# Batch operands of a seven-product layer: their order, their pairing, and one quarter summed in place

## The chip, the cores and the metric

The kernel runs on one core of a Trainium2 chip. Its metric is the device time of one execution in microseconds (us). The engines are named as in the profile: PE is TensorE (PEld its weight loads), DVE is VectorE, ACT is ScalarE, POOL is GpSimd, SP is SyncE, which issues most DMAs. Each engine works through its own list of instructions in order; they wait for each other by semaphores.

## The reference

Three layers follow each other. First an attention in two steps over 4 batches, 8 heads, 576 positions and 64 channels, then two feed-forward layers on 2304 tokens of 512 channels:

```python
p_packed = sm_attn(p, k, v)              # 32 packed queries per head
out = sm_attn(q, p_packed, p_packed)
x = out.transpose(0, 2, 1, 3).reshape(2304, 512)
h = x @ w_in                              # 512 x 2048
x = (np.maximum(h, 0) + np.log1p(np.exp(-np.abs(h)))) @ w_out
gate = 1 / (1 + np.exp(-(x @ w_gate)))    # 512 x 1536, "the second layer"
val = x @ w_val
return (gate * val) @ w_out2
```

All is float32. The kernel makes a float32 product out of three faster ones: every operand is split into a high part (a rounded copy) and a low part (the operand minus its high part), and high x high, high x low and low x high are summed.

## The kernel before, in words

**Stages.** Attention units and the first layer overlap from the start; the first layer ends at about 436 us of the profile, and the second layer fills the rest. Its input is `xa`, the first layer's sum, kept in SBUF transposed: per batch two halves of 288 positions (x1, x2), each with 512 channels.

**The second layer as seven products.** Gate and value are not computed as two products of 512 channels. Per batch the input is cut into four quarters of 256 channels x 288 positions, A11 and A12 (the two channel halves of x1), A21 and A22 (of x2), and the weights likewise; seven products of 256 channels are formed instead of eight (Winograd's variant of Strassen's method). On the input side it needs seven operands: A11, A12, A22, and the sums S1 = A21 + A22, S2 = S1 - A11, S3 = A11 - A21, S4 = A12 - S2. A21 itself is in no product. Each operand is 128 x 576 (two blocks of 128 channels by 288 positions).

**Making the operands.** `prep_A(b)` is a generator; each `yield` ends one step. A quarter is "split": ACT copies it to the high part (line 698), then DVE (for A22 POOL) subtracts to get the low part (line 99). A sum is one DVE instruction (line 705) into a tile `sum`, of which there is one buffer. Operands are allocated in pairs, one tile for both high parts and one for both low parts, the pairs being (A11, A12), (A22, S1), (S2, S3) and S4 alone. The tiles of batches 2 and 3 take the places of those of batches 0 and 1, and a tile is free only when both operands in it have had their last product.

**The loops.** `ps` is 0 for batches 0 and 1, then 1 for batches 2 and 3; inside, `f` runs over 12 slices of the hidden channels. `emit_gv` forms the seven products for each f in the order A11, S2, S3, S1, A12, A22, S4. Per operand and batch a product is 6 matmuls of 288 columns (lines 111 to 113), so one f is 84. The results gather in three PSUM banks (`ps_m`, pairs of banks); DVE adds them (lines 927 and 939) and each bank is free again only when DVE or ACT has read it. `emit_out2` is the last product: per pair of slices nine blocks of 6 matmuls of 512 columns (lines 974 to 976), each added into `xa` by DVE (line 982); two PSUM tiles serve these. After the last pair of each `ps` the sums go out by DMA (line 991).

**What sets the order.** Work that prepares later stages hangs in a queue `jobs`, and each call of `tick()` (after every product and block) takes one step from its front. `prep_B` makes the weight operands of the next f: DVE converts the raw weights in three steps each (lines 178, 183, 187), ACT and POOL split them. `prep_A(0)` and `prep_A(1)` enter the queue near the end of the first layer. The last f of ps 0 is run batch by batch: when batch 0's products are emitted, `prep_A(2)` goes to the front of the queue, and after batch 1's, `prep_A(3)` goes to the front, ahead of what is left of `prep_A(2)`. A scheduler then fixes every engine's list: it moves instructions forward past others where data and buffers allow. So `sum` of batch 2 already stands at 437 us, and the place of an instruction follows from both.

The stretch from about 616 to 655 us, in which ps 0 ends and the operands of batches 2 and 3 are made, is called the turn below.

Of the kernel before, what the change touches and what calls it, by code (L numbers as in the profile page):

```python
# [9 lines left out]
F32 = mybir.dt.float32  # L10
# [3 lines left out]
ALU = mybir.AluOpType  # L14
# [6 lines left out]
def attn_moe_moe_kernel(  # L21
# [21 lines left out]
    nc = tc.nc  # L43
# [5 lines left out]
    P = 128  # L49
# [241 lines left out]
    SPL = []  # L291
    SP0 = []
    ALO = ['A22']
    EV2 = EM2 = EM1 = [nc.vector, nc.vector]
    EGL = [nc.gpsimd, nc.vector]
    HIA = [5, 9]
# [382 lines left out]
    HB = B // 2  # L679
    Aop, Bop, scratch, gv = {}, {}, {}, {}  # L680

    def prep_A(b):
        pool = w2[0] if b % 2 == 0 else big
        n = 11 if pool is big else 7
        Aop[b] = {}
        for nms in (("A11", "A12"), ("A22", "S1"), ("S2", "S3"), ("S4",)):
            tiles = [
                pool.tile([P, 2, 2, HS], F32R, tag="big", bufs=n, name="aop")
                for _ in range(len(nms))
            ]  # L690
            for e, nm in enumerate(nms):
                Aop[b][nm] = [tiles[0][:, e], tiles[-1][:, 1 if len(nms) == 1 else e]]
        x11, x12 = x2(b, 0)[:, :2], x2(b, 0)[:, 2:]
        x21, x22 = x2(b, 1)[:, :2], x2(b, 1)[:, 2:]

        def split(nm, x):
            hi, lo = Aop[b][nm]
            nc.scalar.activation(hi, x, AF.Copy)
            split_lo(nc.gpsimd if nm in ALO else nc.vector, lo, x, hi)

        def sum_():
            return w2[0].tile([P, 2, HS], F32, tag="sum", name="sum")

        def tt(to, x, y, op):
            nc.vector.tensor_tensor(to, x, y, op=op)

        split("A11", x11)
        yield
        split("A12", x12)
        yield  # L710
        split("A22", x22)
        yield
        t = sum_()
        tt(t, x21, x22, ALU.add)
        yield
        split("S1", t)
        yield
        tt(t, t, x11, ALU.subtract)
        yield
        split("S2", t)  # L720
        yield
        tt(t, x12, t, ALU.subtract)
        yield
        split("S4", t)
        yield
        t = sum_()
        tt(t, x11, x21, ALU.subtract)
        yield
        split("S3", t)
        yield  # L730


# [99 lines left out]
    for i, (b, c) in enumerate(entries):  # L832
        if c == 0:
            while not att_done(2 * b + 1):
                att_tick()
            if b:
                for cc in range(2):
                    jobs.appendleft((f"wp{b}{1 - cc}", prep_wp_one(b, 1 - cc)))
        if (b, c) == (3, 0):
            jobs.append(("win2", prep_win(2)))  # L840
        if (b, c) == (3, 1):
            jobs.append(("wp02", prep_wp_two(0, 2)))
        if c >= 2 and b % 2 == 0:
            k = groups.index((b // 2, c))
            if k == 0:
                jobs.append(("wo2", prep_wo(2)))
            if k + 1 < len(groups):
                x, cc = groups[k + 1]
                jobs.append((f"wp{2 * x}{cc}", prep_wp_two(x, cc)))
            if k + 2 < len(groups) and weights and groups[k + 2][1] == weights[0]:  # L850
                cc = weights.popleft()
                jobs.extend(idle)
                idle.clear()
                jobs.append((f"win{cc}", prep_win(cc)))
                jobs.append((f"wo{cc}", prep_wo(cc)))
                idle.append((f"early{cc}", prep_early(early_in.get(cc, ()))))
            if (b, c) == BAT:
                jobs.extend(idle)
                idle.clear()
                jobs.append(("B00", prep_B(0, 0)))  # L860
        for x in range(2):
            if (b, c) == (x + 2, NCH1 - 2):
                jobs.append((f"A{x}", prep_A(x)))
        if (b, c) == CPC:
            cps[0] = CPS > 0
        if (b, c) == (1, 2):
            att.release()
            w2.append(tc.alloc_tile_pool(name="w2", bufs=1, side="right"))
        finish(f"wp{b}{c}" if c < 2 else f"wp{b - b % 2}{c}")
        for s in range(2):  # L870
            emit_h(b, c, s)
            pace = 0
            for bb in range(b + 1, B if c < 2 else 0):
                slots = 3 * (4 * bb - 2 * i - s) - MARGIN
                pace = max(pace, -(-att_left(2 * bb + 1) // max(1, slots)))
            ticks = [pace] * 3
            if len(pend) == DEPTH:
                emit_out1(*pend.popleft(), ticks)
            else:
                for m in range(KD):  # L880
                    between(m, ticks)
            pend.append((b, c, s))
# [119 lines left out]
    for i, (ps, f) in enumerate(steps):  # L1002
        finish(f"B{ps}{f}")
        if i + 1 < len(steps):
            n_ps, n_f = steps[i + 1]
            jobs.append((f"B{n_ps}{n_f}", prep_B(n_ps, n_f)))
        whole = list(range(HB))
        first_last = f in (SPL if ps else (SP0 + [NF - 1]))
        for n, group in enumerate([[p] for p in whole] if first_last else [whole]):
# [46 lines left out]
```

## Time and profile before

| what | value |
| --- | --- |
| median of three runs (lowest, highest) | 868.61 us (866.66, 870.32) |
| the profiled execution, its span | 866.77 us, 864.7 us |
| busy: PE, DVE, POOL, ACT | 839.6, 614.6, 473.2, 401.1 us |
| granted TensorE clock, mean | 1.000 of full speed |
| HBM read, written | 65.67 MB, 18.87 MB |

The span runs from the first to the last instruction; 2.07 us of the profiled time lie outside it. Busy times are of the engine's own instructions. A matmul's modelled duration is longer than the distance to the next one, since matmuls are pipelined: PE can count as busy while it loses time, and the loss is seen in the distances between starts. In the rows further down a line gives start, duration, engine, line of the kernel, operation, output tile <- input tiles, shapes and count.

### The profile page before, as it was taken

What the parts mean: (1) busy time and instruction counts of PE and PEld (TensorE: products, weight loads), DVE (VectorE), ACT (ScalarE), POOL (GpSimd) and SP (SyncE); (2) the same over time, 40 slices, a digit from 0 to 9 for tenths busy, and PEclk for the clock granted to TensorE, in tenths of its full rate; (3) what the DMA queues carried; (4) which work ended last, traced back from release to release, by engine and by line L of the source; (5) the groups of instructions that cost most, each with busy time, mean ns of one, the idle gap of its engine ahead of it and who ended that gap; (6) DMA issues with size and microseconds to landing.
All of it is one profiled execution on the core that took longest, in us unless ns stands there. A gap on an engine that the chain in (4) does not pass through costs nothing.

```text
span 864.7 us, 15615 instructions
## 1 busy us (share of the span) xinstructions
PE 839.6 (97%) x6100; PEld 789.6 (91%) x6100; DVE 614.6 (71%) x1047; ACT 401.1 (46%) x721; POOL 473.2 (55%) x455
## 2 busy tenths in 40 slices
PE   6899999999999999999999999999989999999997
PEld 5788999989999999999999999999869999999995
DVE  1875556757576767758898688897898756767665
ACT  4567565566666666677633422232342532322210
POOL 4454233346565545576479787796883634536400
PEclk9999999999999999999999999999999999999999
DMA  9983330113032402300057464554434212213004
GB/s 233 229 221 84 80 83 2 50 49 99 1 98 92 135 21 79 123 30 1 1 167 215 134 192 148 170 136 157 140 95 137 79 45 86 67 43 111 14 1 109
DMA packets 58009, 85.55 MB, mean 99 GB/s; under 512 B 6352, under 2 KB 39248, under 8 KB 57936
## 3 DMA queue, kind: packets, MB, share of 16 engines
q1 hardware_dynamic: 57648, 84.49, 34.5%
q8 instruction: 48, 0.79, 0.4%
q14 instruction: 25, 0.20, 0.1%
q10 hardware_dynamic: 288, 0.07, 0.0%
HBM read 65.67 MB, written 18.87 MB: 98 GB/s over the span
## 4 chain that ended last, share of the span: by engine, by line
PE 84%; DVE 7%; DMA 3%; ACT 2%; POOL 2%; issue 1%; SPq 0%; POOLq 0%; ACTq 0%; DVEq 0%
PE bank L113 9%; PE bank L111 9%; PE bank L112 9%; PE ps L650 7%; PE ps L651 7%; PE ps L653 7%; PE ps L976 5%; PE ps L975 5%; PE ps L974 5%; PE ps L113 4%; PE ps L111 4%; PE ps L112 4%; PE ps L587 2%; DVE aop L99 2%; PE ps L464 2%; PE ps L348 1%
## 5 line engine op out<-in xcount | busy, mean ns | idle before, releaser
L111 PE MATMUL bank<-aop,BH 128*128 128x288 f32 x672 | 198.7, 296 | 2.8 <-DVE work L927 1.1
L112 PE MATMUL bank<-aop,BH 128*128 128x288 f32 x672 | 197.9, 295 | 1.0 <-DVE aop L99 0.9
L113 PE MATMUL bank<-aop,BL 128*128 128x288 f32 x672 | 198.7, 296 | 0.1
L99 POOL TENSOR_TENSOR ghl<-g,ghl 128x576 fp32r<-128x576 f32 x64 | 93.7, 1464 | 131.5 <-ACT ghl L106 131.5
L658 DVE TENSOR_TENSOR xa<-xa,ps 128x288 f32<-128x288 f32 x224 | 98.1, 449 | 75.4 <-PE ps L653 75.3
L650 PE MATMUL ps<-ghl,woh 128*128 128x288 f32 x512 | 148.6, 305 | 1.6 <-DVE xa L658 1.5
L651 PE MATMUL ps<-ghl,wol 128*128 128x288 f32 x512 | 143.2, 295 | 0.0
L111 PEld LDWEIGHTS bank<-aop,BH 128*128 128x128 f32 x672 | 126.2, 188 | 8.0 <-issue 1.2
L112 PEld LDWEIGHTS bank<-aop,BH 128*128 128x128 f32 x672 | 126.4, 188 | 5.1 <-DVE aop L99 1.6
L113 PEld LDWEIGHTS bank<-aop,BL 128*128 128x128 f32 x672 | 126.5, 188 | 0.4 <-POOL BL L99 0.4
L99 POOL TENSOR_TENSOR BL<-cv,BH 128x512 fp32r<-128x512 f32 (+1 forms) x96 | 117.7, 1242 | 7.2 <-ACT BH L106 6.1
L653 PE MATMUL ps<-ghl,woh 128*128 128x288 f32 x512 | 109.1, 294 | 0.0
L650 PEld LDWEIGHTS ps<-ghl,woh 128*128 128x128 f32 x512 | 96.2, 188 | 4.1 <-DVE xa L658 1.3
L651 PEld LDWEIGHTS ps<-ghl,wol 128*128 128x128 f32 x512 | 96.3, 188 | 0.6
L927 DVE TENSOR_TENSOR work<-work,bank 128x576 f32<-128x576 f32 (+1 forms) x100 | 70.9, 724 | 28.6 <-PE bank L113 28.1
L974 PE MATMUL ps<-oh,gv 128*128 128x512 f32 x216 | 84.6, 392 | 1.3 <-DVE xa L982 0.8
L975 PE MATMUL ps<-ol,gv 128*128 128x512 f32 x216 | 84.8, 393 | 0.0
L976 PE MATMUL ps<-oh,gv 128*128 128x512 f32 x216 | 84.7, 393 | 0.0
L653 PEld LDWEIGHTS ps<-ghl,woh 128*128 128x128 f32 x512 | 82.2, 188 | 0.0
L982 DVE TENSOR_TENSOR xa<-xa,ps 128x512 f32<-128x512 f32 x90 | 61.5, 684 | 27.1 <-PE ps L976 26.6
L956 ACT ACTIVATE work<-bank 128x576 f32<-128x576 f32 (+1 forms) x25 | 15.8, 634 | 137.4 <-DVE bank L927 137.4
L113 PE MATMUL ps<-A2h,wpl 128*128 128x288 f32 x256 | 76.2, 297 | 2.4 <-POOL wpl L99 2.0
(123 smaller groups left out, 1743.6 us busy)
## 6 DMA issues: line engine op xcount, KB each, us to landing
cv<-B SPq DMA_DIRECT2D x52, 256.0 KB, 2.6
B<-cv SPq DMA_DIRECT2D x48, 256.0 KB, 3.8
raw_in<-in_moe_w_in_dram SPq DMA_DIRECT2D x16, 512.0 KB, 3.6
raw_out<-in_moe_w_out_dram SPq DMA_DIRECT2D x16, 512.0 KB, 3.6
raw_g<-in_moe_w_gate_dram SPq DMA_DIRECT2D x12, 512.0 KB, 4.2
raw_v<-in_moe_w_val_dram SPq DMA_DIRECT2D x12, 512.0 KB, 4.4
raw_o<-in_moe_w_out_dram SPq DMA_DIRECT2D x12, 512.0 KB, 4.1
xa<-in_q_dram SPq DMA_DIRECT2D x6, 576.0 KB, 6.5
```

The costliest lines, as they stand in the source:

```text
L99: eng.tensor_tensor(lo, x, hi.bitcast(F32), op=ALU.subtract)
L111: nc.tensor.matmul(ps, wh, xh, start=first, stop=False)
L112: nc.tensor.matmul(ps, wh, xl, start=False, stop=False)
L113: nc.tensor.matmul(ps, wl, xh, start=False, stop=last)
L650: nc.tensor.matmul(out_, wh[:, ms], gh[:, f], start=f == 0, stop=False)
L651: nc.tensor.matmul(out_, wl[:, ms], gh[:, f], start=False, stop=False)
L653: nc.tensor.matmul(out_, wo_hl[c, f][0][:, ms], gl[:, f], start=False, stop=f == 1)
L658: nc.vector.tensor_tensor(dst, dst, out_, op=ALU.add)
L927: nc.vector.tensor_tensor(to, x, y, op=ALU.add)
L974: nc.tensor.matmul(bank, gh[:, ts_], oh, start=f == 0, stop=False)
L975: nc.tensor.matmul(bank, gh[:, ts_], ol, start=False, stop=False)
L976: nc.tensor.matmul(bank, gl[:, ts_], oh, start=False, stop=f == 1)
```

## The change

Three things are altered in `prep_A`, and one is added.

- Before the splits a new generator `fold_A(b)` overwrites A21 in `xa` by two DVE instructions: A21 + A22, then minus A11. What stands there afterwards is S2.
- The operands are then made in the order A11, S2, S3, S1, A12, A22, S4, which is the order of the products. S2 is split from `xa` itself. The others come from it: S3 = A22 - S2, S1 = S2 + A11, S4 = A12 - S2, one DVE instruction each.
- The pairs are (A11, S2), (S3, S1), (A12, A22) and S4 alone.
- `fold_A(0)` and `fold_A(1)` enter the queue just ahead of `prep_A(0)` and `prep_A(1)`; `fold_A(2)` and `fold_A(3)` enter it at f = 3 and f = 5 of ps 0.

Per batch that is 2 folding sums and 3 sums where there were 4 sums; the splits are the same seven. The core of the diff:

```diff
+    FOLD = {3: 2, 5: 3}
+    def fold_A(b):
+        x11, x12, x21, x22 = quarters(b)
+        tt(x21, x21, x22, ALU.add)
+        yield
+        tt(x21, x21, x11, ALU.subtract)
+        yield
     def prep_A(b):
-        for nms in (("A11", "A12"), ("A22", "S1"), ("S2", "S3"), ("S4",)):
+        for nms in (("A11", "S2"), ("S3", "S1"), ("A12", "A22"), ("S4",)):
...
         split("A11", x11)
         yield
+        split("S2", s2)
+        yield
+        t = sum_(x22, s2, ALU.subtract)
+        yield
+        split("S3", t)
+        yield
+        t = sum_(s2, x11, ALU.add)
+        yield
+        split("S1", t)
+        yield
         split("A12", x12)
         yield
         split("A22", x22)
         yield
-        t = sum_()
-        tt(t, x21, x22, ALU.add)
-        yield
-        split("S1", t)
-        yield
-        tt(t, t, x11, ALU.subtract)
-        yield
-        split("S2", t)
-        yield
-        tt(t, x12, t, ALU.subtract)
+        t = sum_(x12, s2, ALU.subtract)
         yield
         split("S4", t)
-        yield
-        t = sum_()
-        tt(t, x11, x21, ALU.subtract)
-        yield
-        split("S3", t)
         yield
...
             if (b, c) == (x + 2, NCH1 - 2):
+                jobs.append((f"F{x}", fold_A(x)))
                 jobs.append((f"A{x}", prep_A(x)))
...
+        if ps == 0 and f in FOLD:
+            jobs.append((f"F{FOLD[f]}", fold_A(FOLD[f])))
```

In the lists that follow, a row is line, operation, output <- inputs and shape; line numbers of the changed kernel are higher by 1 to 13 (658 is 659, 705 is 688, 927 is 939, 939 is 951, 974 is 986, 982 is 994). First DVE's list at the end of the first layer, from the split of S4 of batch 1; `xa<-xa,ps` with a number adds one of the first layer's last blocks, `raw_g` is the first weight conversion of f = 1. Before:

```order
L99 TENSOR_TENSOR aop<-sum,aop 128x576
L658 TENSOR_TENSOR xa<-xa,ps_5441 128x288
L632 SCALAR_TENSOR_TENSOR g_5449<-ps_5405,t_5418 128x576
L705 TENSOR_TENSOR sum<-xa 128x576
L658 TENSOR_TENSOR xa<-xa,ps_5456 128x288
L658 TENSOR_TENSOR xa<-xa,ps_5466 128x288
L99 TENSOR_TENSOR aop<-sum,aop 128x576
L658 TENSOR_TENSOR xa<-xa,ps_5474 128x288
L658 TENSOR_TENSOR xa<-xa,ps_5482 128x288
L658 TENSOR_TENSOR xa<-xa,ps_5490 128x288
L658 TENSOR_TENSOR xa<-xa,ps_5498 128x288
L178 TENSOR_SCALAR ps_5556<-raw_g 128x512
```

And in the changed kernel, from the split of S1 of batch 1:

```order
L99 TENSOR_TENSOR aop<-sum,aop 128x576
L659 TENSOR_TENSOR xa<-xa,ps_5441 128x288
L633 SCALAR_TENSOR_TENSOR g_5449<-ps_5404,t_5417 128x576
L659 TENSOR_TENSOR xa<-xa,ps_5456 128x288
L659 TENSOR_TENSOR xa<-xa,ps_5466 128x288
L688 TENSOR_TENSOR sum<-xa 128x576
L99 TENSOR_TENSOR aop<-xa,aop 128x576
L659 TENSOR_TENSOR xa<-xa,ps_5476 128x288
L99 TENSOR_TENSOR aop<-sum,aop 128x576
L659 TENSOR_TENSOR xa<-xa,ps_5486 128x288
L659 TENSOR_TENSOR xa<-xa,ps_5494 128x288
L659 TENSOR_TENSOR xa<-xa,ps_5502 128x288
```

Behind the block 5441 the changed list has three sums or splits (S4's sum, A12, S4) where before has two (S3's sum, S3).

Next DVE's list inside the turn. `work` and `bank` are the sums of the products, `ps1` with a number is a block of the last product, `aop` an operand's tile. Before, the last rows up to the split of S3 of batch 2 (aop_7785), which is the last operand made; aop_7868 is S4 and aop_7867 S3 of batch 3:

```order
L705 TENSOR_TENSOR sum_7875<-xa_78,sum_7875 128x576
L927 TENSOR_TENSOR work_7931<-work_7908,bank_7932 128x576
L982 TENSOR_TENSOR xa_78<-xa_78,ps1_8096 128x512
L99 TENSOR_TENSOR aop_7868<-sum_7875,aop_7868 128x576
L982 TENSOR_TENSOR xa_78<-xa_78,ps1_8127 128x512
L705 TENSOR_TENSOR sum_7885<-xa_78 128x576
L982 TENSOR_TENSOR xa_78<-xa_78,ps1_8168 128x512
L99 TENSOR_TENSOR aop_7867<-sum_7885,aop_7866 128x576
L982 TENSOR_TENSOR xa_78<-xa_78,ps1_8194 128x512
L705 TENSOR_TENSOR sum_7892<-xa_78 128x576
L982 TENSOR_TENSOR xa_78<-xa_78,ps1_8220 128x512
L99 TENSOR_TENSOR aop_7785<-sum_7892,aop_7784 128x576
```

In the changed kernel, where aop_7874 holds S1, aop_7876 A12 and aop_7877 S4 of batch 3, and sum_7900 belongs to S4 of batch 2:

```order
L688 TENSOR_TENSOR sum_7886<-xa_78 128x576
L951 TENSOR_TENSOR work_7829<-work_7829,bank_7844 128x288
L939 TENSOR_TENSOR bank_7858<-work_7798,bank_7858 128x288
L99 TENSOR_TENSOR aop_7876<-xa_78,aop_7875 128x576
L951 TENSOR_TENSOR work_7842<-work_7842,bank_7858 128x288
L99 TENSOR_TENSOR aop_7874<-sum_7886,aop_7873 128x576
L688 TENSOR_TENSOR sum_7894<-xa_78 128x576
L939 TENSOR_TENSOR work_7939<-work_7916,bank_7940 128x576
L99 TENSOR_TENSOR aop_7877<-sum_7894,aop_7877 128x576
L939 TENSOR_TENSOR work_7958<-work_7939,bank_7959 128x576
L688 TENSOR_TENSOR sum_7900<-xa_78 128x576
L939 TENSOR_TENSOR work_7939<-work_7939,bank_7975 128x576
```

Before, five blocks of the last product (ps1) stand in these rows; now none does, and in their place stand the sums of the first products of ps 1: S2, S3 and S1 (bank_7940, bank_7959, bank_7975).

Last, PE's list at the turn. `bank<-aop` rows are the seven products, `ps1` rows the nine blocks of the last pair of ps 0. Before, behind the product S2 of batch 2 (aop_7784, aop_7785):

```order
L111 MATMUL bank_7932<-aop_7784,BH_7656 128x288
L112 MATMUL bank_7932<-aop_7785,BH_7656 128x288
L113 MATMUL bank_7932<-aop_7784,BL_7657 128x288
L976 MATMUL ps1_8012<-oh_7336,gv_7449 128x512
L974 MATMUL ps1_8012<-oh_7538,gv_7628 128x512
L975 MATMUL ps1_8012<-ol_7539,gv_7628 128x512
L976 MATMUL ps1_8012<-oh_7538,gv_7629 128x512
L974 MATMUL ps1_8040<-oh_7336,gv_7448 128x512
L975 MATMUL ps1_8040<-ol_7337,gv_7448 128x512
L976 MATMUL ps1_8040<-oh_7336,gv_7449 128x512
```

In the changed kernel, behind the product A22 of batch 3 (aop_7875, aop_7876):

```order
L111 MATMUL bank_8007<-aop_7875,BH_7664 128x288
L112 MATMUL bank_8007<-aop_7876,BH_7664 128x288
L113 MATMUL bank_8007<-aop_7875,BL_7665 128x288
L986 MATMUL ps1_8020<-oh_7546,gv_7636 128x512
L987 MATMUL ps1_8020<-ol_7547,gv_7636 128x512
L988 MATMUL ps1_8020<-oh_7546,gv_7637 128x512
L111 MATMUL bank_8035<-aop_7794,BH_7664 128x288
L112 MATMUL bank_8035<-aop_7794,BH_7664 128x288
L113 MATMUL bank_8035<-aop_7794,BL_7665 128x288
```

Before, 18 matmuls of ps 1 (A11 of both batches, S2 of batch 2) run, then all nine blocks with S2 of batch 3 between them, then S3 and the rest. In the changed list 72 matmuls of ps 1 (A11, S2, S3, S1, A12, A22, all for both batches) run with no block between them, then half a block, then S4; the other eight blocks stand behind that, spread over the products of f = 1. The 18 output DMAs of ps 0 follow their blocks: in SP's list they now stand among the loads of weights for f = 3 and f = 4 of ps 1, where before they stood in one piece ahead of these. DVE's two folding sums of batch 2 stand at the start of f = 0 of ps 0, those of batch 3 in f = 1 and f = 2, earlier than they enter the queue; the sum for S3 of batch 2 stands in f = 2, where before the sum for S1 of batch 2 stood at the start of f = 0.

## Rows read from the trace of the kernel before

**Rows 1.** The page's first part: busy time, share, instructions.
```profile
PE 839.6 (97%) x6100; PEld 789.6 (91%) x6100; DVE 614.6 (71%) x1047; ACT 401.1 (46%) x721; POOL 473.2 (55%) x455
```

**Rows 2.** PE's waits at the turn, 619 to 660 us: total, times, longest.
```profile
PE bank L111 <- DVE work L927: 1.1, 2, 0.8
PE bank L112 <- DVE aop L99: 0.9, 1, 0.9
PE ps L974 <- DVE xa L982: 0.8, 1, 0.8
PE bank L111 <- DVE work L939: 0.6, 1, 0.6
```

**Rows 3.** PE's waits at the first layer's end, 420 to 437 us.
```profile
PE ps L650 <- DVE xa L658: 1.5, 3, 0.6
PE bank L111 <- DVE xa L658: 0.7, 1, 0.7
```

**Rows 4.** PE's waits from 437 to 480 us.
```profile
PE bank L111 <- POOL ol L99: 0.5, 1, 0.5
```

**Rows 5.** PE matmuls with operand tiles by stretch: elapsed, busy (count), clock, DMA share, GB/s.
```profile
436.14:442.10 5.96, 5.96 (x46) 1.00 0.65 179
627.59:653.50 25.91, 10.32 (x66) 1.00 0.43 126
```

**Rows 6.** The same for matmuls of the last product, `gv`.
```profile
645.80:653.54 7.74, 7.73 (x34) 1.00 0.81 257
627.80:653.50 25.70, 13.00 (x54) 1.00 0.43 127
```

**Rows 7.** The same for the first layer's last blocks, `ghl`.
```profile
423.26:435.90 12.64, 10.46 (x72) 1.00 0.00 0
```

**Rows 8.** DVE groups by shape, 619 to 653.55 us: busy, mean ns, idle before.
```profile
L99 DVE TENSOR_TENSOR aop<-sum,aop 128x576 fp32r<-128x576 f32 x8 | 8.3, 1038 | 0.7 <-ACT aop L698 0.5
...
L99 DVE TENSOR_TENSOR aop<-xa,aop 128x576 fp32r<-128x576 f32 x4 | 5.7, 1434 | 0.1
L705 DVE TENSOR_TENSOR sum<-xa 128x576 f32<-128x576 f32 x3 | 3.3, 1110 | 0.0
...
L705 DVE TENSOR_TENSOR sum<-xa,sum 128x576 f32<-128x576 f32 x2 | 2.4, 1181 | 0.0
...
L705 DVE TENSOR_TENSOR sum<-sum,xa 128x576 f32<-128x576 f32 x2 | 1.5, 744 | 0.0
```

**Rows 9.** DVE's instructions in order of time, inside the turn.
```profile
616.82 0.45 DVE L927 TENSOR_TENSOR work<-work,bank 128x288 f32<-128x288 f32 x1 [0.20 <-PE bank L113]
...
636.86 0.44 DVE L939 TENSOR_TENSOR work<-work,bank 128x288 f32<-128x288 f32 x1
637.23 0.45 DVE L927 TENSOR_TENSOR bank<-work,bank 128x288 f32<-128x288 f32 x1
...
641.11 0.68 DVE L982 TENSOR_TENSOR xa<-xa,ps 128x512 f32<-128x512 f32 x1
641.71 0.74 DVE L705 TENSOR_TENSOR sum<-sum,xa 128x576 f32<-128x576 f32 x1
642.38 0.67 DVE L982 TENSOR_TENSOR xa<-xa,ps 128x512 f32<-128x512 f32 x1
643.20 1.78 DVE L99 TENSOR_TENSOR aop<-sum,aop 128x576 fp32r<-128x576 f32 x1 [0.15 <-ACT aop L698]
```

**Rows 10.** POOL's instruction that runs beside DVE's last one of rows 9.
```profile
643.09 1.28 POOL L99 TENSOR_TENSOR BL<-cv,BH 128x512 fp32r<-128x512 f32 x1
```

**Rows 11.** DVE groups at the first layer's end, 423.26 to 435.91 us.
```profile
L99 DVE TENSOR_TENSOR aop<-sum,aop 128x576 fp32r<-128x576 f32 x3 | 3.7, 1235 | 0.7 <-ACT aop L698 0.6
...
L183 DVE SCALAR_TENSOR_TENSOR ps<-raw_g,ps 128x512 int32<-128x512 int32 x1 | 0.7, 679 | 0.0
```

**Rows 12.** Busy by stretch: elapsed, then PE, PEld, DVE, ACT, POOL, clock, DMA share, GB/s.
```profile
436.00:460.00 24.00, 23.52 (x176) 23.31 (x177) 22.39 (x35) 8.77 (x13) 21.61 (x26) 1.00 0.69 200
460.00:600.00 140.00, 139.87 (x895) 130.51 (x895) 114.98 (x175) 40.67 (x66) 111.52 (x124) 1.00 0.56 164
```

More of the change, by code (lines that the diff above doesn't have):

```diff
@@ L680, in attn_moe_moe_kernel, with quarters, tt @@
     Aop, Bop, scratch, gv = {}, {}, {}, {}
+    def quarters(b):
+        x1, x2_ = x2(b, 0), x2(b, 1)
+        return x1[:, :2], x1[:, 2:], x2_[:, :2], x2_[:, 2:]
+    def tt(to, x, y, op):
+        nc.vector.tensor_tensor(to, x, y, op=op)
+    def fold_A(b):
[4 more added lines that the diff above has]
+        yield
     def prep_A(b):
@@ L692, in prep_A @@
                 Aop[b][nm] = [tiles[0][:, e], tiles[-1][:, 1 if len(nms) == 1 else e]]
-        x11, x12 = x2(b, 0)[:, :2], x2(b, 0)[:, 2:]
-        x21, x22 = x2(b, 1)[:, :2], x2(b, 1)[:, 2:]
+        x11, x12, s2, x22 = quarters(b)
         def split(nm, x):
@@ L699, in split, with sum_ @@
             split_lo(nc.gpsimd if nm in ALO else nc.vector, lo, x, hi)
[L701 to L705, printed above, removed]
+        def sum_(x, y, op):
+            t = w2[0].tile([P, 2, HS], F32, tag="sum", name="sum")
+            tt(t, x, y, op)
+            return t
         split("A11", x11)
+        yield
[8 more added lines that the diff above has]
+        split("S1", t)
         yield
```

## The prediction

> **What bounds the kernel now.** I read the page's first part, then PE's waits by stretch, then the distances between PE's starts, then DVE's groups where PE loses time. PE is busy 839.6 of 864.7 us and no other engine passes 71% [rows 1]: only time that PE loses can be won, and the change must win it where it acts. A matmul of 288 columns follows the one before in 5.96 / 45 = 0.1324 us (the 46th of that row was already running), one of 512 columns in 7.74 / 34 = 0.2276 [rows 5, 6]. With that I can say what a stretch needs. At the turn, from 627.59 to 653.55, PE runs 66 matmuls of seven products and 54 of the last product [rows 5, 6]: 66 x 0.1324 + 54 x 0.2276 = 21.0 us in 25.96, so 4.9 us are lost. The waits that the profile names there are all for DVE, 3.4 us together, and only one of 0.9 us is for an operand; the others are for banks and blocks that DVE has not yet read [rows 2]. At the first layer's end 72 matmuls need 9.5 us and take 12.65 until the first of the second layer starts [rows 7]: 3.1 lost, again to DVE [rows 3]. From 437 on one wait of 0.5 us is for POOL, at the first change of weights [rows 4]. So about 8.5 us lie where operands are made, and there DVE is the engine that is late.
>
> **The turn: what goes, what comes.** DVE makes 12 low parts (two more are POOL's) and 7 sums there now, in 21.2 us, the five groups summed [rows 8]. One of these by itself takes 0.74 and the next starts 0.67 later (641.71 to 642.38) [rows 9]. One that meets a POOL instruction takes far longer: the split of 643.20 ends at 644.98, 0.61 after POOL's instruction of 643.09 ended at 644.37 [rows 9, 10]. So DVE was held until POOL was through. Over the 19, the excess above 0.745 is 21.2 - 14.2 = 7.0 us, 0.37 each.
>
> The change leaves 17: both folding sums of batches 2 and 3 and the sum for S3 of batch 2 are made long before, and two of the old sums have gone. It also lets DVE begin earlier. A11 and S2 of batch 2 take the tiles of A11 and S2 of batch 0, and the product S2 has been read by 616.82 + 0.37 [rows 9], while the first split used to start behind two more products. Against that stands what PE's list now asks. Before, all nine blocks (12.3 us of PE) stood in front of the product S3 and covered the making of S1, S4 and S3. Now 72 matmuls of ps 1 and half a block run first. The blocks are not lost, but they come when the operands are no longer wanted.
>
> I work out when the last operand is ready. From 616.8 to the split of S4 of batch 2 DVE's list has 18 sums of half banks at 0.37 (636.86 to 637.23), 5 blocks at 0.60 (641.11 to 641.71), 4 sums of whole banks and 17 splits and sums at 0.67 each (a whole bank has an operand's 576 columns) [rows 9]: 6.7 + 3.0 + 2.7 + 11.4 = 23.8 us. I followed POOL's list beside it, holding each of the 17 until POOL's current instruction ends and POOL's until DVE's ends: 0.40 each, 6.8 us, and 0.6 of waits for ACT and PE. DVE is through at 616.8 + 31.2 = 648.0. PE wants that operand after batch 1's 42 matmuls, six of a block and 72 of ps 1: 627.59 + 5.6 + 1.4 + 9.5 = 644.1. The loss is 3.9 where it was 4.9: **-1.0 us**.
>
> The ends: if POOL never held DVE, it would be through at 641.2 and nothing would be lost, -4.9. If each of the 17 took the 1.434 us of the four slowest splits [rows 8], 0.69 above one alone, the excess is 11.7 and DVE is through at 652.9, a loss of 8.8, +3.9. I take the worked value, since it is nearest to the 0.37 of the 19 measured.
>
> A rule of the Trainium skill bears on this: SBUF — State Buffer, section "Who interferes with whom", says that a VectorE instruction with two SBUF inputs and a GpSimd instruction that reads SBUF exclude each other, whoever starts second waiting for the whole of the other. The trace agrees (644.37 and 644.98). It speaks against the change in one point: the folding sums have two SBUF inputs as well, so each can hold POOL or be held wherever it is put. Were it a plain slowdown, the mean of 0.37 would carry over, and DVE would be through at 616.8 + 23.8 + 6.3 + 0.6 = 647.5, the turn at -1.5 in place of -1.0.
>
> **The first layer's end.** For batches 0 and 1 the change adds one DVE instruction each (2 folds and 3 sums for 4 sums). Batch 0's falls where DVE has room. Of batch 1's work the folds and the first sum come early, but A12 and S4 are now split last: behind block 5441 stand three splits or sums where there were two, while one conversion step moves behind the last block. A split costs 1.235 there, one conversion step 0.68 [rows 11]: +0.6 for the last block. The third conversion step of the value weights, on which POOL's first run for f = 1 waits (the 0.5 of [rows 4]), has the full instruction more ahead of it, +1.2. PE can lose both only once: I take **+0.9**. The ends: the three splits in that stretch are partly held by POOL now, and if the new places avoid POOL, 3 x (1.235 - 0.745) = -1.5; if the three behind block 5441 are all held like the slowest kind [rows 8], 3 x 0.69 = +2.1.
>
> **Folds in f = 0 to 2.** Four folding sums and one sum in place of one sum: 4 x 0.67 = 2.7 us of DVE. From 460 to 600 DVE is busy 115 of 140 us and PE loses nothing to speak of, so two of them cost nothing; from 436 to 460 it is 22.4 of 24 [rows 12], so the two of batch 2 fit barely. I take **+0.2**, between 0 and 1.3 (two in full); if DVE's room were gone, each would delay a bank by 0.67.
>
> **Transfers.** Nothing is added. The 18 output DMAs of ps 0 now wait for blocks that run through f = 1 of ps 1, and the loads for f = 3 queue behind some of them. These weights are wanted only when f = 2 has run too, at least 84 x 0.1324 = 11 us after the last such block, and that cover hides them; without it, PE would wait for as much as a load is late.
>
> **Sum.** -1.0 + 0.9 + 0.2 = +0.1 on the profiled 866.77 us. Of this 864.7 is the span; the 2.07 outside stay. The median of the runs is 1.84 above the profiled one, so I forecast on its scale: 868.61 + 0.1 = **868.7 us**, and by the bounds of the likely terms (turn -2.5 to +1.5, the rest 0 to +2) 866.1 to 872.1.
>
> **The rivals.** *The turn is cured.* All of PE's waits at the turn are for DVE [rows 2]; with two sums fewer and an earlier start DVE might give its banks back in time. Then the 4.9 go, the first layer's end costs nothing, and +0.2 stays: 863.9 us. For it speaks that POOL has no more to do than before; against it that POOL must not hold DVE at all. *The cover is missed* (the other side). PE reaches S3 and S1 of batch 3 with no block to fill, and DVE is still held by POOL, every split 1.434: +3.9 + 0.9 + 0.2 = 873.6 us. It decides at the product S1 of batch 3: PE is there 627.59 + 5.6 + 0.7 + 42 x 0.1324 = 639.5 at the earliest, and each us that its split ends later is lost. For it speaks that four of 12 splits now take as long; against, that the others take 1.04. *The order is not what PE waits for.* Three of four waits are for banks, and a bank is freed by DVE's place in its list: the splits stand between the sums as before, and the loss stays 4.9, only elsewhere: 0 + 0.9 + 0.2 = 869.7 us.
>
> **How the numbers follow.** Forecast 0.52, order not the cause 0.20, turn cured 0.18, cover missed 0.10. What a measurement of this kernel can tell from no change is 0.5%, 4.3 us: faster is below 864.3, slower above 872.9. Only the cured turn reaches below, and with little to spare (0.14 of its 0.18); only the missed cover reaches above, with most of its share (0.08). That gives 0.14, 0.78 and 0.08. The range of eight in ten holds forecast and third rival, and reaches towards the cured turn: 864.0 to 872.2.
>
> **What would show it.** In the new trace PE should run the first six products of ps 1 in one piece from about 636, with waits for DVE of 3 to 5 us in all between 627 and 650, the last of them for the split of S4 or S1, and no block before 645. DVE's last split should end near 648, ahead of eight of the nine blocks instead of among them. At the first layer's end PE's first product should start up to 1 us later than 435.9. Wrong would be: no waits at the turn (cured), a single wait above 2 us before S3 or S1 (cover missed), a DVE idle at the turn, or a wait for weights in f = 2 to 4 of ps 1.

## The result, and the profile after

The changed kernel takes 873.35 us in the median of 6 runs (873.13 to 876.75), the kernel before 868.55 in the same comparison: a ratio of 1.0067, with a 95% interval of 1.0053 to 1.0080. It is slower, by 4.8 us, and lies above the range of 864.0 to 872.2. The profiled execution took 874.09 us, its span is 872.2.

The page's first part, the row that answers to [rows 1]:

```profile
PE 843.1 (97%) x6100; PEld 791.7 (91%) x6100; DVE 619.0 (71%) x1051; ACT 400.1 (46%) x721; POOL 476.1 (55%) x455
```

Totals do not show where the time went. I cut the second layer, and the last part of the first, at instructions that both kernels have: the sum `g` of the first layer that is the 20th from the last, ACT's copies of the bank of A11, and its sigmoids. The rows of these cuts, first before, then after (start, duration, engine, line; ACT's copy of an operand, line 698 before, is line 714 in the changed kernel):

```profile
328.43 0.75 DVE L632 SCALAR_TENSOR_TENSOR g<-ps,t 128x576 f32<-128x576 f32 x1
437.81 0.65 ACT L944 ACTIVATE work<-bank 128x576 f32<-128x576 f32 x1 [0.63 <-PE bank L113]
471.05 0.65 ACT L956 ACTIVATE work<-bank 128x576 f32<-128x576 f32 x1
600.15 0.65 ACT L944 ACTIVATE work<-bank 128x576 f32<-128x576 f32 x1 [1.90 <-PE bank L113]
840.18 0.65 ACT L956 ACTIVATE work<-bank 128x576 f32<-128x576 f32 x1 [10.62 <-DVE bank L927]
```

```profile
329.26 0.75 DVE L633 SCALAR_TENSOR_TENSOR g<-ps,t 128x576 f32<-128x576 f32 x1
444.61 0.65 ACT L956 ACTIVATE work<-bank 128x576 f32<-128x576 f32 x1 [8.79 <-PE bank L113]
481.10 0.65 ACT L968 ACTIVATE work<-bank 128x576 f32<-128x576 f32 x1 [1.23 <-DVE bank L939]
609.85 0.65 ACT L956 ACTIVATE work<-bank 128x576 f32<-128x576 f32 x1 [1.90 <-PE bank L113]
847.60 0.65 ACT L968 ACTIVATE work<-bank 128x576 f32<-128x576 f32 x1 [10.62 <-DVE bank L939]
```

These are the start of the first layer's end, the first product of the second layer (f = 0 of ps 0), the sigmoid of f = 2, the first product of f = 10, and the last sigmoid of ps 1. Before, the four stretches between them take 109.38, 33.24, 129.10 and 240.03 us; after, 115.35, 36.49, 128.75 and 237.75. So the first layer's end lost 5.97, f = 0 to 2 lost 3.25, f = 3 to 9 won 0.35, and the turn won 2.28. The sum is 6.6; 0.83 more lies ahead of the first cut. The medians differ by 4.8 and the two profiles by 7.3; run 12 below shows how far the part ahead of that cut varies by itself.

**The turn.** PE's waits from 619 to 670 us, the rows that answer to [rows 2]:

```profile
PE bank L111 <- ACT work L956: 0.6, 1, 0.6
PE ps L986 <- DVE xa L994: 0.5, 1, 0.5
PE bank L111 <- DVE work L939: 0.4, 1, 0.4
PE bank L112 <- DVE aop L99: 0.2, 1, 0.2
```

1.7 us where there were 3.4, and 0.2 of them for an operand; 0.6 is for ACT, the rest for DVE. I had forecast waits of 3 to 5 us. The turn does what the change says, and more of it than I forecast.

**The first layer's end.** PE's waits from 423 to 443 us, which answer to [rows 3], and the busy time of three stretches ahead of that, before and after (elapsed, then PE, PEld, DVE, ACT, POOL, granted clock):

```profile
PE ps L651 <- DVE xa L659: 1.7, 3, 0.8
PE ps L654 <- POOL ghl L99: 0.7, 1, 0.7
PE bank L111 <- DVE xa L659: 0.5, 1, 0.5
```

```profile
388.00:396.00 8.00, 8.00 (x57) 7.79 (x57) 7.25 (x10) 6.04 (x10) 5.23 (x3) 1.00 0.00 0
396.00:404.00 8.00, 8.00 (x63) 8.00 (x62) 7.54 (x13) 6.20 (x10) 4.67 (x4) 1.00 0.00 0
404.00:412.00 8.00, 8.00 (x63) 8.00 (x62) 5.01 (x11) 5.31 (x8) 4.29 (x4) 1.00 0.01 2
```

```profile
388.00:396.00 8.00, 8.00 (x59) 7.84 (x59) 7.50 (x12) 5.88 (x11) 2.73 (x2) 1.00 0.00 0
396.00:404.00 8.00, 6.51 (x48) 6.23 (x47) 7.97 (x11) 6.42 (x11) 6.25 (x6) 1.00 0.00 0
404.00:412.00 8.00, 6.88 (x51) 6.53 (x50) 7.15 (x10) 2.72 (x5) 4.16 (x3) 1.00 0.01 2
```

Before, DVE is busy 14.8 of the 16 us from 388 to 404 and rests after it, and PE runs through. After, DVE is full until 411 and PE lies idle 2.6 us. What DVE does there, and what POOL does beside it:

```profile
402.72 1.27 DVE L99 TENSOR_TENSOR aop<-sum,aop 128x576 fp32r<-128x576 f32 x1
403.92 3.74 DVE L688 TENSOR_TENSOR xa<-xa 128x576 f32<-128x576 f32 x2
...
407.95 0.75 DVE L688 TENSOR_TENSOR sum<-xa 128x576 f32<-128x576 f32 x1
...
409.35 0.74 DVE L633 SCALAR_TENSOR_TENSOR g<-ps,t 128x576 f32<-128x576 f32 x1
```

```profile
403.34 1.95 POOL L99 TENSOR_TENSOR ghl<-g,ghl 128x576 fp32r<-128x576 f32 x1
405.25 1.80 POOL L99 TENSOR_TENSOR wpl<-cv,wph 128x512 fp32r<-128x512 f32 x1
```

The two folding sums of batch 1 take 3.74 us, 1.87 each in the mean, where one alone takes 0.75. They end at 407.66, 0.61 after POOL's second instruction at 407.05: the same 0.61 as in the split of [rows 9, 10]. The sum `g` stands behind them in DVE's list; before, its counterpart came 5.78 us earlier (403.57), 4.95 when the 0.83 ahead of the first cut are taken off. ACT, POOL and PE wait for it in turn.

**The granted clock.** Five rows of the same view, 1 us each:

```profile
438.00:439.00 1.00, 0.16 (x3) 0.02 (x1) 1.00 (x3) 0.00 (x0) 0.00 (x0) 0.72 0.00 0
439.00:440.00 1.00, 1.00 (x4) 1.00 (x5) 1.00 (x3) 0.00 (x0) 0.00 (x0) 0.50 0.00 0
440.00:441.00 1.00, 1.00 (x6) 1.00 (x5) 0.19 (x2) 0.00 (x0) 0.00 (x0) 0.50 0.00 0
441.00:442.00 1.00, 1.00 (x6) 0.88 (x4) 0.88 (x2) 0.00 (x0) 0.00 (x0) 0.58 0.00 0
442.00:443.00 1.00, 0.45 (x3) 0.34 (x3) 0.84 (x2) 0.00 (x0) 0.00 (x0) 1.00 0.00 0
```

For the last blocks PE ran at 1.2 in place of 2.4 GHz. Its longest wait just before was 0.8 us (the waits above); of the 4 us from 435 to 439 it was busy for 2.0. The parts below full speed add up to 0.28 + 0.50 + 0.50 + 0.42 = 1.7 us. No stretch from 425 to 480 of the profile before has a clock below 1.00.

### The profile page after: what moved, and what is told of

It reads as the page before. It is cut to its first block, busy times and chain, and to the rows that moved or that the text cites. A ratio compares the mean times of both kernels' runs of the same rounds, so it can differ in the third digit from the quotient of the medians.

```text
span 872.2 us, 15622 instructions
## 1 busy us (share of the span) xinstructions
PE 843.1 (97%) x6100; PEld 791.7 (91%) x6100; DVE 619.0 (71%) x1051; ACT 400.1 (46%) x721; POOL 476.1 (55%) x455
```

## The experiments

For each run the table gives the median, the ratio to the kernel before, and how much longer than before the four stretches were (cut as above, from the run's own profile; the two clock columns give what the lower clock took in the first two stretches and in the last, summed as above, and are contained in the stretches).

| kernel | median us | ratio, 95% interval | first layer's end | f = 0 to 2 | f = 3 to 9 | turn to end | clock, first two | clock, turn |
| --- | --- | --- | --- | --- | --- | --- | --- | --- |
| changed | 873.35 | 1.0067 (1.0053 to 1.0080) | 5.97 | 3.25 | -0.35 | -2.28 | 1.70 | 0 |
| 1: 0, 1 old making, new pairs | 870.79 | 1.0022 (1.0013 to 1.0031) | 0.83 | 3.45 | -0.36 | -1.82 | 0 | 0 |
| 2: 2, 3 old making, new pairs | 877.00 | 1.0095 (1.0081 to 1.0110) | 5.69 | 1.31 | 0.34 | 1.90 | 1.71 | 1.71 |
| 3: old order in 0, 1 | 874.45 | 1.0078 (1.0056 to 1.0099) | 5.13 | 3.32 | -0.35 | -2.18 | 0 | 0 |
| 4: folds of 2, 3 late | 874.00 | 1.0058 (1.0041 to 1.0076) | 5.92 | 1.93 | 0.37 | -2.16 | 1.70 | 0 |
| 5: folds of 0, 1 on POOL | 878.41 | 1.0108 (1.0091 to 1.0126) | 9.20 | 3.02 | -0.29 | -2.15 | 1.70 | 0 |
| 6: folds of 1 later | 874.43 | 1.0068 (1.0055 to 1.0081) | 5.08 | 3.47 | -0.36 | -2.19 | 1.70 | 0 |
| 7: 0, 1 wholly old, folds late | 868.81 | 1.0001 (0.9991 to 1.0011) | 0.10 | 0.18 | 0.01 | 1.52 | 0 | 1.71 |
| 8: new pairs alone | 870.23 | 1.0026 (1.0014 to 1.0038) | 1.05 | -0.14 | 0.00 | 1.90 | 0 | 1.71 |
| 9: as 7, new pairs in 0 | 867.38 | 0.9987 (0.9968 to 1.0005) | 0.01 | 0.29 | 0.01 | -1.72 | 0 | 0 |
| 10: two-input dummies | 875.69 | 1.0080 (1.0053 to 1.0107) | 4.50 | 3.34 | 0.34 | -0.56 | 1.71 | 0 |
| 11: one-input dummies | 875.50 | 1.0076 (1.0046 to 1.0106) | 5.79 | 1.92 | 0.36 | -0.54 | 0 | 0 |
| 12: before once more | 871.10 (1 run) | | 0.02 | -0.06 | 0.00 | -0.03 | 0 | 0 |

Theory 1, from the two profiles: the first layer's end pays for the extra sums and the late splits of batches 0 and 1, f = 0 to 2 for the folds of batches 2 and 3, and the turn gains.

**Run 1, batches 0 and 1 made in the old way.**

```diff
-        split("A11", x11) ... split("S4", t)      # for batches 0 and 1
+        A11, A12, A22, t = A21 + A22: S1, t -= A11: S2, t = A12 - t: S4, t = A11 - A21: S3
-                jobs.append((f"F{x}", fold_A(x)))
```

> The order, sums and products of batches 2 and 3 as in the changed kernel, those of batches 0 and 1 as in the kernel before (four sums each, no folding beforehand, A12 and A22 split early); tiles paired as changed. Theory 1 (the loss is batches 0 and 1: about 5.8 us by the end of the first layer, 3.2 from the folding sums that stand in VectorE's list where it has no room, 2.6 from splits that are now last and meet GpSimd; the turn gains 2 to 3; the folds of batches 2 and 3 cost about 2 in the first f steps): 873.4 - 5.8 = 867.6 us, between 866.5 and 868.7; last block of the first layer within 1 us of 435.9. Rival (the first layer's difference in the one profile is run variation, the loss is in the second layer): 872 to 874, as the changed kernel.

The first layer's end fell from 5.97 to 0.83: the loss there belongs to batches 0 and 1, and is no variation from run to run. But the time is 870.8, not 867.6: f = 0 to 2 kept their whole loss although the layer ended in time, and I had put 2 on it.

**Run 2, batches 2 and 3 made in the old way, no folds for them.**

> Batches 0 and 1 as in the changed kernel, batches 2 and 3 with the order and sums of the kernel before and no folding beforehand for them (tiles paired as changed). Theory 1: the first layer's loss of 5.8 stays, the 2 us of the first f steps go, the turn loses 2 to 3 us more than the changed kernel: 873.4 - 2.0 + 2.5 = 873.9, between 872.8 and 875.2. Rival (the loss is in the second layer, through the folds of batches 2 and 3): 868 to 870.

Slower than the changed kernel, by more than expected. The first layer's loss stays. f = 0 to 2 lose 1.31 with no fold in them, so part of that loss comes from the late layer. And the turn is not as it was before but 1.9 worse, with the new pairs and the old order; I had overlooked that the pairs had stayed new. Of these 1.90 us 1.71 are lower clock, from 663 to 668 us: without it the turn would be 0.2 longer, near to what it was before.

**Run 3, the folds of batches 0 and 1, but their splits in the old order** (A11, A12, A22, S1, S2, S4, S3, the sums all from the folded A21).

> As the changed kernel, with the folding sums of batches 0 and 1 too, but these two batches' operands made in the old order (A11, A12, A22, S1, S2, S4, S3). It tells the extra and moved sums from the new order of the splits. Theory 1 (both count, 3.2 for the sums and 2.6 for the order): 873.4 - 2.6 = 870.8, between 869.8 and 871.8. Rival 'order alone': as with the old making throughout, 867.6. Rival 'sums alone': 873.4.

The rival "sums alone" (873.4) is the nearest: 5.13 against 5.97, the time the same as the changed kernel's within the intervals. The order of the splits is not the cause. The changed kernel's 5.97 holds 1.70 of lower clock and run 3's 5.13 none, so without it the new order is the shorter by 0.9.

**Run 4, the folds of batches 2 and 3 late.**

```diff
-    FOLD = {3: 2, 5: 3}
+    FOLD = {7: 2, 9: 3}            # and both instructions kept in program order
```

> As the changed kernel, with the folding sums of batches 2 and 3 pinned at f = 7 and f = 9 of ps 0, where PE loses nothing, in place of f = 0 to 2. Theory 1 (these folds cost about 2 us where they stand): 873.4 - 2.0 = 871.4, between 870.5 and 872.3, and no waits for DVE at 445 to 480 beyond 1.2 us. Rival (the loss of f = 0 to 2 comes from the first layer ending late and the converted weights with it, not from the folds): 873.4, no change.

f = 0 to 2 got 1.3 shorter, f = 3 to 9 got 0.7 longer (0.37 against -0.35), and the time did not change beyond its interval. PE's waits there were 0.9 for POOL's low part of the weights and 0.9 for DVE. With run 1, where the layer ended in time and the folds alone lost 3.45, and run 2, where there were no folds and 1.31 were lost: either cause is enough, and they don't add.

**Run 5, the folds of batches 0 and 1 made by POOL.**

```diff
-        tt(x21, x21, x22, ALU.add)
+        nc.gpsimd.tensor_tensor(x21, x21, x22, op=ALU.add)     # b < 2; the second likewise
```

> As the changed kernel, but the folding sums of batches 0 and 1 are made by GpSimd in place of VectorE (those of batches 2 and 3 stay). Theory 1 (the folding sums cost what they add to VectorE's time from 388 to 410, where it has no room: two-input work of 16.7 us there against 12.3 before, and 4.3 us of the 5.1 lost by the fourth g from the end): the first product of the second layer starts at most 2.5 us later than before, against 6.0; 873.4 - 4 = 869.4 us, between 868.4 and 871. Rival (GpSimd's own work, gh and the weights' low parts, is what the folds hold up, and it would now be later still): 873 or more.

Theory 1 missed. The rival's number came in (873 or more) and its mechanism did not: PE's only wait for POOL there is 0.7 us. The two POOL sums of batch 1 took 1.42 and 1.40 us, as those of batch 0 did, and yet the first layer lost 9.2, of them 1.70 by the clock. DVE's waits from 386 to 456 us of this run:

```profile
DVE sum L688 <- POOL xa L696: 9.5, 2, 5.1
DVE xa L659 <- PE ps L654: 7.8, 8, 1.9
```

DVE itself stood for 9.5 us at two sums that need the folded A21, with the blocks and the next `g` queued behind them. A fold that is late on another engine costs more here than a fold on DVE.

**Run 6, the same instructions, the folds of batch 1 some 20 places later in DVE's list.**

> As the changed kernel, with the same instructions, but the two folding sums of batch 1 pinned some 20 places later in VectorE's list, behind the g that they stood in front of, where VectorE has room (4.4 of 8 us busy at 412 to 420 in the changed kernel). Theory 1 (place, not number): the 3.3 us that are lost between the g at 401 and the one at 409 go, some come back at the last blocks, since all of batch 1's operands are made later: 873.4 - 2.5 = 870.9, between 870 and 872. Rival (the number of instructions decides, wherever they stand): 873.4.

At the `g` before which they had stood the loss was indeed gone (0.5 us there, against 4.95), but at the layer's end it had come back: 5.08. Of these 1.70 are again lower clock, now at 432 to 436. Without the lower clock it is 3.4 against 4.3, and the time is the changed kernel's, as the rival said. The run does not show that no place is free: DVE is busy only 9.2 of the 16 us from 404 to 420, but the folds ran at 419.80 and 421.18, at the head of eight us in which it is busy throughout. A place between 409 and 419 was not tried.

**Run 7, batches 0 and 1 as before in every point, folds of 2 and 3 late.**

> Batches 0 and 1 as in the kernel before in every point (order, sums, tiles paired); batches 2 and 3 as changed, with their folding sums pinned at f = 7 and 9. Theory 1: the first layer's end costs nothing (within 0.3 us of before), f = 0 to 2 at most 1, the pinned folds 0.4, the turn gains 1.5 to 2.3: 868.6 - 1 = 867.6, between 866.5 and 868.6, faster than both kernels. Rival (the turn's gain hangs on the tile pairs of batches 0 and 1: with the old ones the first tiles of batch 2 come free only after the product A12): 869 to 870.

The rival was right that the turn's gain hangs on the pairs; 868.81 lies between the two ranges, 0.2 from either. The losses of the first three stretches are gone, the pinned folds cost nothing (0.18 and 0.01), but the turn lost 1.52 in place of gaining. There PE waited for operands (1.3 for ACT's high part, 0.9 for DVE's low part): with A11 and A12 of batch 0 in one pair, batch 2's first tiles come free only after the product A12. Behind these waits the clock fell (1 us each, the granted clock is third from the end):

```profile
651.00:652.00 1.00, 0.60 (x3) 0.55 (x3) 1.00 (x3) 0.42 (x1) 0.00 (x0) 0.74 0.00 0
652.00:653.00 1.00, 1.00 (x6) 1.00 (x5) 0.66 (x1) 0.24 (x1) 0.00 (x0) 0.50 0.13 39
653.00:654.00 1.00, 1.00 (x6) 1.00 (x5) 0.00 (x0) 0.39 (x1) 0.00 (x0) 0.50 0.76 223
654.00:655.00 1.00, 1.00 (x4) 0.88 (x4) 0.51 (x1) 0.75 (x2) 0.62 (x1) 0.55 0.00 0
```

That is 0.26 + 0.50 + 0.50 + 0.45 = 1.71 us: without it the turn would be 0.2 shorter than before, hardly a gain and no loss. Five of the twelve runs have a mean granted clock of 1.000, and their median is 867.96 us, where that of the nine such runs of the kernel before in the same comparison is 867.53.

**Run 8, the pairing alone.**

```diff
-        for nms in (("A11", "A12"), ("A22", "S1"), ("S2", "S3"), ("S4",)):
+        for nms in (("A11", "S2"), ("S3", "S1"), ("A12", "A22"), ("S4",)):
```

> The kernel before with nothing but the new pairing of operands in tiles (A11 with S2, S3 with S1, A12 with A22), for all batches; order and sums as before, no folding beforehand. It tells what the pairing alone does. With the old making of batches 0 and 1 and the new pairs the first layer ended 0.8 us later; with the old order in batches 2 and 3 and the new pairs the turn lost 1.9 us more than before: 868.6 + 0.8 + 1.9 = 871.3, between 870.3 and 872.3. Rival (pairing has no cost of its own, those two came from the folding sums): 868.6.

The two stretches came as expected, 1.05 and 1.90, but the second for another reason: 1.71 of the 1.90 are lower clock, from 657 to 661 us. The time is just below the range. f = 0 to 2 lost nothing (-0.14), so the pairs do not cost there. In DVE's list the pairing moves one split of batch 1, A12, six places down: its tiles are now the fifth and sixth of the batch and no longer the first two.

**Run 9, put together from these.**

```diff
+        old = (("A11", "A12"), ("A22", "S1"), ("S2", "S3"), ("S4",))
+        for nms in (old if b == 1 else new):      # making of 0 and 1 as before, folds late
```

> Batches 0 and 1 made as in the kernel before (order, sums, no folding); batch 0's tiles paired as changed, batch 1's as before; batches 2 and 3 as changed, their folding sums pinned at f = 7 and 9. Theory 2 (after seven runs: the first layer's end pays for VectorE's added time and for batch 1's new pairs, f = 0 to 2 for the folds that stand there, and the turn's gain needs the tiles of A11 and S2 of batch 0 in one pair): first product of the second layer within 0.3 us of before, f = 0 to 2 within 0.3, the turn -2.3: 868.5 - 2.0 = 866.5, between 865.6 and 867.4. Rival (the turn's gain hangs on the pairs of batch 1 too): 868.5 to 870.

As expected in the first three stretches, 0.01, 0.29 and 0.01; the turn won 1.72 where 2.3 were expected. 867.38 against 868.10 in the same comparison, clearly below the changed kernel; below the kernel before by median, with an interval (0.9968 to 1.0005) that still holds no change.

**Runs 10 and 11, superfluous work where the folds are queued.**

```diff
+        tt(x21, x21, x21, ALU.max)                                   # run 10: twice for batches 0 and 1
+        nc.vector.tensor_scalar(x21, x21, 1.0, None, op0=ALU.mult)   # run 11: in its place
```

> The kernel before with two superfluous VectorE instructions each for batches 0 and 1, where the changed kernel queues its folding sums: in-place maxima of A21 with itself (two inputs from SBUF, 576 columns), which change no value. Theory 2 (VectorE has no room at the first layer's end, and each added instruction costs its time there with what GpSimd holds it): 4 x 1.25 (27.4 us over 22 instructions of this kind in the changed kernel) = 5.0 us by the first product of the second layer, 868.5 + 5.0 = 873.5, between 872 and 874.5. Rival (the changed kernel loses by where it puts the making of operands, not by added time): 868.5 to 869.5.

> As the run with the superfluous maxima, but in-place multiplications of A21 by one: one input from SBUF in place of two, the same 576 columns, two each for batches 0 and 1. Theory 2 with the hold: a one-input instruction is not held by GpSimd, so each costs 0.75 us at most and the four 3.0 or less: 871.5 or less, at least 1.5 below the run with two inputs. Rival (the hold does not matter, only the count): the same time as with two inputs.

Run 10: 4.50 at the first layer's end where 5.0 were expected (0.42 of them lower clock); what the time has beyond the range is f = 0 to 2 (3.34, of which 1.3 is the part of the lower clock that falls after 443.8), which I had left out. Run 11 did not come out lower, and my premise was wrong. One of its instructions alone takes 0.45 us, but two of the four took over three times that. DVE's rows, then POOL's:

```profile
391.14 0.45 DVE L695 TENSOR_SCALAR xa<-xa 128x576 f32<-128x576 f32 x1
...
405.31 1.55 DVE L693 TENSOR_SCALAR xa<-xa 128x576 f32<-128x576 f32 x1
406.90 1.58 DVE L695 TENSOR_SCALAR xa<-xa 128x576 f32<-128x576 f32 x1
```

```profile
404.75 1.80 POOL L99 TENSOR_TENSOR wpl<-cv,wph 128x512 fp32r<-128x512 f32 x1
406.51 1.65 POOL L99 TENSOR_TENSOR ghl<-g,ghl 128x576 fp32r<-128x576 f32 x1
```

They end 0.31 and 0.32 after POOL's ends (406.55 and 408.16): held like the others. The Trainium skill says so in SBUF — State Buffer, section "Who interferes with whom": a scalar operation with one input can run in a mode that takes the port shared with GpSimd, and is then shut out as well. The trace agrees, 0.45 against 1.55. So these two runs show that added DVE instructions are enough for the loss (no operand was moved or changed), but do not tell the hold from the count.

**Run 12, the kernel before once more.**

> The kernel before once more, for a second profile: which stretches vary from one execution to another by themselves. By each theory the distances from the sums g at the first layer's end to the end of the program are the same within 0.3 us, and what differs lies before them: 867 to 870.

All four stretches are the same within 0.06 us, yet the run is 871.1, above the range. All of its difference lies ahead of the first cut, 4.40 us, of which 1.71 are lower clock (182 to 187 us). So the stretches can be compared between single profiles, with the lower clock taken out where it falls into one; the totals of single profiles can't.

## Why the prediction was wrong

**The first layer's end was the step that failed: +0.9 forecast, bounds -1.5 to +2.1, 5.97 measured.** I wrote that batch 0's extra instruction "falls where DVE has room" and that batch 1's folds "come early". They did come early, and batch 0's landed at 388, batch 1's at 404, within and right behind a stretch in which DVE had no room: busy 14.8 of 16 us. I had opened only the stretch from 420 on [rows 3, 7, 11], in which the old kernel visibly waits, and had taken the stretch before it for free because PE lost nothing there. With DVE almost full, PE did not wait before, and did with the next instructions. The parts, by the runs and if they add up: the new pairs of batch 1 1.05 (run 8, and 0.01 where batch 1 kept the old ones, run 9); the folds about 4.1 (5.13 - 1.05, run 3; the dummies of run 10, with the old pairs, also cost 4.1 without their 0.42 of lower clock); the lower clock 1.70, for which my sum had no term; the new order about -0.9 (what is left). The price of an instruction was wrong too: I took 0.75 to 1.24. From 380 to the end of the layer the sums and splits take, in groups, before and after:

```profile
L99 DVE TENSOR_TENSOR aop<-sum,aop 128x576 fp32r<-128x576 f32 x8 | 8.2, 1024 | 3.0 <-ACT aop L698 2.9
L705 DVE TENSOR_TENSOR sum<-xa 128x576 f32<-128x576 f32 x5 | 4.7, 949 | 0.1
L99 DVE TENSOR_TENSOR aop<-xa,aop 128x576 fp32r<-128x576 f32 x4 | 4.5, 1144 | 1.4 <-ACT aop L698 1.4
L705 DVE TENSOR_TENSOR sum<-sum,xa 128x576 f32<-128x576 f32 x2 | 3.4, 1682 | 0.0
L705 DVE TENSOR_TENSOR sum<-xa,sum 128x576 f32<-128x576 f32 x2 | 2.4, 1180 | 0.0
```

```profile
L99 DVE TENSOR_TENSOR aop<-xa,aop 128x576 fp32r<-128x576 f32 x6 | 8.9, 1500 | 0.6 <-ACT aop L714 0.6
L688 DVE TENSOR_TENSOR xa<-xa 128x576 f32<-128x576 f32 x5 | 7.1, 1415 | 0.1
L99 DVE TENSOR_TENSOR aop<-sum,aop 128x576 fp32r<-128x576 f32 x6 | 6.6, 1108 | 0.8 <-ACT aop L714 0.6
L688 DVE TENSOR_TENSOR sum<-xa 128x576 f32<-128x576 f32 x6 | 5.4, 898 | 0.1
```

21 instructions and 23.2 us before, 23 and 28.0 after (one in each list is of batch 2). Two instructions more are 4.8 us more: 1.5 by their own length, 3.3 because the group was held longer (1.22 us in the mean against 1.10). It did not meet POOL more often: 12 end 0.60 to 0.62 us after an instruction of POOL in either profile, but they exceed 0.745 by 0.91 in the mean, where before it was 0.63.

**f = 0 to 2: +0.2 forecast, bounds 0 to 1.3, 3.25 measured.** I priced the folds as DVE time against DVE's idle time. What they hit is a chain that I had not followed: a raw weight is loaded again only when conversion steps on DVE are through, and SP issues the load behind stores of converted weights that wait for POOL. Up to f = 2 nothing but the folds and the pairs differ in run 1, and the pairs alone cost nothing there (run 8). In run 1 the conversion of a raw value weight starts 27.13 us after the stretch's first copy (438.83), before 25.08 after it (437.81), and the whole of DVE's list stands at its load, 2.08 us in place of 0.58. The issue on SP (before, it took 1.41 us by itself) and DVE's wait, before and run 1:

```profile
457.65 1.41 SPq L155 DMA_DIRECT2D raw_v<-in_moe_w_val_dram  x1
...
462.89 0.70 DVE L178 TENSOR_SCALAR ps<-raw_v 128x512 int32<-128x512 int32 x1 [0.58 <-DMA raw_v<-in_moe_w_val_dram]
```

```profile
461.38 0.39 SPq L155 DMA_DIRECT2D raw_v<-in_moe_w_val_dram  x1
...
465.96 0.69 DVE L178 TENSOR_SCALAR ps<-raw_v 128x512 int32<-128x512 int32 x1 [2.08 <-DMA raw_v<-in_moe_w_val_dram]
```

A late first layer goes with the same wait: runs 2, 4, 11 and 10, which have no fold there, lost 1.31, 1.93, 1.92 and (without the lower clock) 2.0 us, and DVE stood 1.7 to 2.7 us at this load in them, against 0.6 to 1.2 before and in runs 7, 8, 9 and 12. Why it is 1.3 in one and 2.0 in another, and why both causes together give no more than one, I did not settle.

**The turn: -1.0 forecast, bounds -4.9 to +3.9, -2.28 measured.** The direction and the steps held. PE runs the six products in one piece, no block comes among them, and DVE's last split starts at 655.07, which is 645.4 on the scale of before (minus the 9.70 by which f = 10 began later): it ends at 646.1, and I had 648.0. DVE was held less than the 0.40 per instruction that I took, 0.29 over the 17. The two parts of the change are worth nothing alone: the pairs with the old order lose 1.9 (runs 2 and 8), the order with the old pairs of batches 0 and 1 loses 1.5 (run 7), all three by 1.71 of lower clock, so that 0.2 more, 0.2 more and 0.2 less is left; both together win 1.7 to 2.3. (Runs 10 and 11 won 0.5 with nothing changed there: differences of that size are not resolved.)

**Transfers: 0 forecast.** Nothing at the turn waits for one, as the waits above show, and from 670 us to the end PE waits once, 0.4 us for ACT, as before. From 480 on the changed kernel shows no loss; f = 3 to 9 are 0.35 shorter, which the sum did not have.

**The rivals.** "The cover is missed" gave 873.6 us, next to the measured 873.35, and is wrong all the same: it asked for waits above 2 us before S3 or S1, and the longest at the turn is 0.6. A number alone does not bear out a mechanism. "The order is not what PE waits for" falls with the turn's gain; only two of the four kinds of wait in [rows 2] were for banks, and not three. None of the rivals put the loss where it was: two carried the same +0.9 and +0.2, and the cured turn put the first layer's end at nothing.

**What stays open.** The stretches of the one profile add up to 6.6 us, the medians to 4.8. The kernel before has 4.40 us of play ahead of the first cut by itself, and its profile lay 1.8 below its median. The lower clock does not fall in every run of the changed kernel, and is not needed for the loss: one of the six has a mean granted clock of 1.000, and it took 873.13 us. How often it falls the runs do not tell. Whether a later place of batch 1's folds would have been free was not tried. Whether run 9 beats the kernel before by the 0.1% of its median was not resolved.

## What to carry to other kernels

An engine that is as full in a stretch as DVE was here (14.8 of 16 us) has no room for more work, even where the engine behind it still shows no wait: read the busy share of every stretch into which a change moves work, not only of those that already wait. Price an added VectorE instruction by what such instructions take in that stretch, with what GpSimd holds them, and ask which load is issued only when the work behind it is done. An order of work and the sharing of its buffers are one change: neither half of this one gained at the turn, only both together did. And look at the granted clock of a stretch before giving its time to a cause: one drop was most of what each half seemed to lose.

## What the runs showed of the hardware

The VectorE sums and splits that took over 0.85 us from 380 us to the end of the first layer, 24 in the two profiles together, all ended 0.60 to 0.62 us after the end of an instruction of GpSimd.

At the first layer's end the lower clock came as one stretch of the same size in six of the fourteen profiles (changed, 2, 4, 5, 6, 10), each 1.70 or 1.71 us of lost speed, with waits of PE before it; in run 6 it covers 432 to 436 us. The same 1.71 was lost at the turn of runs 2, 7 and 8, and ahead of the first cut in runs 7 and 12 (from 180 and 182 us); the profiles of runs 3 and 5 lost 5.1 us there. Only the kernel before, 1, 9 and 11 show no such stretch, the last four microseconds of the program apart.

Runs 1, 3, 8 and 11 waited for DVE at the first layer's end too and kept the full clock there. Runs 10 and 11 waited almost alike (1.6, 0.8 and 1.7 us against 1.6, 0.8 and 1.8), and only run 10 lost clock: a few short waits close together can cost 1.7 us more than their own length, or nothing.
